# The first four rows of w1 as blocks, the sums of batch 1 on VectorE, and other costs in the planner's model

## The chip, the cores and the metric

The kernel runs on one core of a Trainium2 chip. The metric is the time of one execution on the device in microseconds (us). PE is the matrix engine (TensorE), DVE is VectorE, ACT is ScalarE, POOL is GpSimd, and SP issues all DMAs.

## The reference

Three blocks follow each other, on 4 batches of 448 tokens with 768 features:

```python
scores = cap * tanh(q @ k.T / 8 / cap)          # 12 heads of 64, per batch
attn = exp(scores - max); attn /= sum(attn) + 1e-9
x = attn @ v                                    # [4, 448, 768]

xn = (x - mean(x)) / sqrt(var(x) + 1e-6) * g_ln # the FFN
x = x + relu(xn @ w_ch1) @ w_ch2                # 768 -> 3072 -> 768

h = relu(x @ w_in); u, v = halves of h          # the gated block, 1024 = 2 * 512
v_s = w_spatial @ layernorm(v) + b_spatial
out = (u * v_s) @ w_out
```

Everything is in float32. The large weights come to the chip as 64-bit floats, in two 32-bit words each.

## The kernel before

**Stages.** The batches go in pairs. The attention of batches 0 and 1 leads the program: 24 heads, two to a step, so that the indices i are 0, 2, .. 22 (i = 12 is the first of batch 1). Then the FFN's first product runs for batches 0 and 1 (`h_units`, 24 rows of w1, of 128 hidden features each), with the attention of batches 2 and 3 and the conversion of w2 beside it. The second product follows in a form with seven products for eight (`y_seven`), then the gated block (`gmlp`), and then the same for batches 2 and 3.

**Precision.** A large product is made of three matmuls in fp32r: a value is split into a high and a low part (`cp` and `sub`), and hi*hi, hi*lo and lo*hi are summed in PSUM. Attention uses plain fp32 matmuls, of which the trace shows two records each.

**Attention that leads.** `lead_s` makes the scores of three chunks of 128 keys, in two pairs of PSUM banks (`twos`) and one more pair (`t3`), and takes tanh and exp on ScalarE into a tile E. The remaining 64 keys of two steps are made together in `lead_st` into a tile et. `lead_v` adds E's chunks on VectorE into s, multiplies by v, copies the result out as x, and sums s over the partitions with a matmul by ones, into a bank `pr`. Two steps share one such bank, except for the last two (i = 20, 22). A last matmul by `sel`, which has ones for one half of the partitions, adds the sums of et. For i in DIRECT (14, 18, 20, 22) E's third chunk isn't added on VectorE but summed by a matmul of its own. The sums go through DRAM to be inverted and spread over partitions (those of i = 22 are inverted in place), and `emit_n` multiplies x by them.

**Layer norm.** For batch 0 `x_done` adds the six x tiles into `acc` on VectorE; `feature_sum` splits acc and sums it over the partitions by two matmuls in fp32r. For batch 1 (MEANS) `direct_sum` sums the six x tiles by six fp32 matmuls. `ln_center` subtracts the mean, multiplies by g, splits each of the six tiles into xn, and adds up the squares; `ln_scale` makes the variance, whose root only scales x and comes in later.

**The first product.** `h_units` takes four rows of w1 first, then two at a time. For each batch and row `h_unit` sums 18 matmuls (six tiles k of three) in one bank. After the first such unit of batch 0 the mean and the centring of batch 1 are put in. The first four rows of w1 are converted and split ahead, during the attention (`make`), two of them into tiles of the pool rs: a Prelu on ScalarE rebases the upper word, VectorE shifts it and puts in the bits of the lower word.

**PSUM.** There are two pairs of banks (`twos`) and two single `banks`; two more single banks come when `t3` is given back after the last step's scores.

**The order.** No engine's order is written out by hand. Every call is recorded with a cost and a latency (`Recorder.record`), in the order of the program; `order` gives each operation a due time from the PE time before it, and `plan` simulates the five engines' queues and hands out, for each engine that is free, the ready operation that is due first, if its tiles fit into the pools. The result is issued in that order. `attend` gives the times, in matmuls of the first product, at which the stages of a head enter the program; `drive` mixes them with `h_units`. AFTER[2] is the part of that product over which the 24 heads of batches 2 and 3 are spread, and `total` is 24 rows by 36 matmuls.

The profile puts every operation on L568, the call in `record`; it is told apart by its tiles. The changed constants are at L37 to L58, `plan` is at L367, `record` at L539, `make` at L724, `value` at L736, `lead_v` at L878, `x_done` at L974, the layer norm at L1102 to L1160, `h_units` at L1795, `attend` at L1829.

Of the kernel before, what the change touches and what calls it, by code (L numbers as in the profile page):

```python
# [42 lines left out]
SECOND = 0  # L43
DIRECT = 14, 18, 20, 22
SQUARES = ()
MEANS = 1,
# [5 lines left out]
REST = 7, 9  # L52
# [4 lines left out]
SWITCH = 0.17  # L57
NEAR = 3.0  # L58
# [168 lines left out]
class Program:  # L227
# [139 lines left out]
    def plan(self, due):  # L367
# [85 lines left out]
        while True:  # L453
            for e in ready:
# [24 lines left out]
                for j, at in succ[i]:  # L479
                    heapq.heappush(events, (max(now, done - at), 1, seq, j))  # L480
                    seq += 1
# [47 lines left out]
class Recorder:  # L529
# [3 lines left out]
    def __getattr__(self, method):  # L533
# [5 lines left out]
        def record(*args, **kw):  # L539
# [24 lines left out]
            if self.name == "V":  # L564
                cost += 0.06 * sum(hasattr(kw.get(k), "tensor") for k in ("scalar", "scalar1", "scalar2"))

# [10 lines left out]
def attn_ffn_gmlp_kernel(  # L577
# [146 lines left out]
    def make(kind, j):  # L724

        with prog.early():

            made[kind, j] = weight(kind, j, [rs.get().rearrange("p a n -> p (a n)") for _ in range(2)]
# [7 lines left out]
    def value(kind, j, home=None, pool=wr):  # L736
# [8 lines left out]
        else:  # L745
# [5 lines left out]
            A.activation(out=t, in_=hi.bitcast(F32), func=ACTF.Prelu, scale=REBASE, alpha=-(2.0 ** 32))  # L751
            if home is None and kind in ("wv", "wu", "wo"):
# [3 lines left out]
            else:  # L756
                V.tensor_scalar(out=ti, in0=ti, scalar1=3, scalar2=None, op0=ALU.logical_shift_left)
                V.scalar_tensor_tensor(out=ti, in0=lo, scalar=29, in1=ti, op0=ALU.logical_shift_right,
# [119 lines left out]
    def lead_v(i):  # L878
# [5 lines left out]
        parts = [s]  # L884
        if i in DIRECT:
            parts.append(E[:, 2])
        else:
            add(s, s, E[:, 2])
        x = xts[b][h // 2]
        todo.append((i, parts, x, et))  # L890
# [15 lines left out]
        if now:  # L906
            with prog.group():
                most = max(len(a) for _, a, _, _ in now)
                for m in range(most + 1):
                    for n, (j, a, _, e) in enumerate(now):  # L910
                        if m < most and m >= len(a):
                            continue
                        for half in range(2):
                            q = (2 * n + half) * width
                            T.matmul(out=pr[q:q + width], lhsT=sel[:, j // 2 % 2, 0:width] if m == most else ones128[:, 0:width],
                                     rhs=(e if m == most else a[m])[:, half], start=m == 0, stop=m == most)
# [57 lines left out]
    def x_done(b, h, x):  # L974
        k = h // 2
        if b in MEANS:
            return
# [133 lines left out]
    def direct_sum(ps, xs):  # L1111

        for k, x in enumerate(xs):
            with prog.group():
                T.matmul(out=ps, lhsT=ones128, rhs=x, start=k == 0, stop=k == KD - 1)

    means = {}

    def ln_mean(b):
        ps = banks.get()[:, 0:S]  # L1120
        if b in MEANS:
# [673 lines left out]
    def h_units(bs):  # L1795

        j0 = 0
        for m in (4, *[2] * (NF // 2 - 2)):
            w = [weight("w1", row(j0 + j)) for j in range(m)]
            mine = {}  # L1800
            for b in bs:
                for j in range(m):
# [4 lines left out]
                    if b in ln and j == 0:  # L1807
                        ln_scale(b)
# [142 lines left out]
```

## Time and profile before

| | |
|---|---|
| median of 3 runs | 1025.92 us (1025.5 to 1026.25) |
| the profiled execution | 1024.53 us |
| its span, first to last instruction | 1022.4 us |
| PE busy | 1006.7 us, 5130 matmuls |
| VectorE busy | 840.0 us, 1447 instructions |
| ScalarE busy | 554.0 us, 850 instructions |
| DMA | 248.71 MB, 70.9% of 16 engines' span |

Times in the trace are counted from the first instruction. A matmul's duration holds its way through the array, so that a stream of them starts at shorter distances than each one takes; "PE busy" is the union of them. Where one row of the timeline is followed by the next row of the same engine, the distance of the two starts is what the first one took of the engine's time.

### The profile page before, as it was taken

To read this page: it belongs to the slowest core of one execution; us is meant where nothing else is said; L and a number is where in the kernel's file an instruction comes from. 1 tells how busy PE (TensorE), PEld (TensorE's weight loads), DVE (VectorE), ACT (ScalarE), POOL (GpSimd) and SP (SyncE) were. 2 spreads that over 40 slices of the span, in tenths; PEclk is the share of its full clock that TensorE was granted. 3 is DMA by queue.
4 is the path that set the end of the run, shared out by engine and by line. 5 is a ranking of instruction groups with operands and counts; after the bars stand their busy time and mean duration, and the time that the engine had idled before them with its cause. 6 is when DMAs were issued, how large, how long until landed. Compare 5 with 4: busy or idle time off the path is not lost.

```text
span 1022.4 us, 15003 instructions
## 1 busy us (share of the span) xinstructions
PE 1006.7 (98%) x5130; PEld 830.9 (81%) x5130; DVE 840.0 (82%) x1447; ACT 554.0 (54%) x850; POOL 17.8 (2%) x21
## 2 busy tenths in 40 slices
PE   7999999999999999999999999999999999999998
PEld 2334687788778889999989899999989999998887
DVE  3869889878868879988889999888788777778996
ACT  7996866776576444455555345444554322214553
POOL 0000000000000000000001110000000000000000
PEclk9999999999999999999999999999999999999999
DMA  6646689999999999989774233566799987602402
GB/s 209 207 142 178 206 283 342 362 353 380 337 346 346 361 346 400 409 321 359 260 249 158 50 132 116 162 202 200 251 332 375 323 261 236 189 23 69 132 16 108
DMA packets 131759, 248.71 MB, mean 243 GB/s; under 512 B 21682, under 2 KB 93540, under 8 KB 131684
## 3 DMA queue, kind: packets, MB, share of 16 engines
q1 hardware_dynamic: 131684, 247.76, 70.9%
q8 instruction: 40, 0.66, 0.2%
q14 instruction: 35, 0.29, 0.1%
HBM read 167.70 MB, written 80.01 MB: 242 GB/s over the span
## 4 chain that ended last, share of the span: by engine, by line
PE 78%; DMA 11%; DVE 4%; ACT 3%; SPq 1%; issue 1%; DVEq 0%; ACTq 0%
PE bank L568 51%; PE two L568 26%; DMA kept_w<-wr 2%; ACT e L568 2%; DMA w<-in_w_dram 2%; SPq L568 1%; DMA hs<-inv 1%; DMA kept_w<-wc 1%; DMA qk<-in_qk_dram 1%; DVE small L568 1%; DMA x<-hs 1%; DMA h<-hx 1%; DVE rs L568 1%; ACT es L568 1%; PE t L568 1%
## 5 line engine op out<-in xcount | busy, mean ns | idle before, releaser
L568 PE MATMUL bank<-rs,wh 128*128 128x448 f32 x1704 | 356.9, 363 | 1.3 <-ACT hs L568 1.3
L568 PEld LDWEIGHTS bank<-rs,wh 128*128 128x128 f32 x1704 | 318.3, 187 | 28.5 <-ACT hs L568 3.7
L568 DVE TENSOR_TENSOR rs<-hs,rs 128x448 fp32r<-128x448 f32 x159 | 94.6, 620 | 3.8 <-ACT rs L568 3.7
L568 PE MATMUL two<-rs,wh 128*128 128x448 f32 x414 | 92.7, 362 | 0.0
L568 ACT ACTIVATE rs<-hs 128x448 fp32r<-128x448 f32 x126 | 68.1, 569 | 31.4 <-DMA hs<-h 25.7
L568 PEld LDWEIGHTS two<-rs,wh 128*128 128x128 f32 x414 | 77.6, 188 | 5.2
L568 DVE TENSOR_TENSOR wh<-wr,wh 128x768 fp32r<-128x768 f32 (+2 forms) x72 | 62.4, 866 | 4.6 <-ACT wh L568 4.2
L568 ACT ACTIVATE wh<-wr 128x768 fp32r<-128x768 f32 (+2 forms) x53 | 40.8, 770 | 30.5 <-DVE wr L568 14.2
L568 ACT ACTIVATE hs<-bank 128x448 f32<-128x448 f32 x56 | 30.1, 540 | 33.0 <-PE bank L568 29.1
L568 ACT ACTIVATE wc<-w 128x512 f32<-128x512 f32 x36 | 24.1, 673 | 38.4 <-DMA kept_w<-wc 20.4
L568 ACT ACTIVATE es<-es,capt 128x896 f32<-128x896 f32 x42 | 42.3, 1048 | 0.0
L568 PE MATMUL two<-qk 64*128 64x448 f32 (+1 forms) x168 | 36.0, 593 | 4.1 <-DMA qk<-in_qk_dram 4.1
L568 ACT ACTIVATE rs<-x 128x448 fp32r<-128x448 f32 x34 | 19.1, 575 | 32.3 <-DVE x L568 31.0
L568 PE MATMUL bank<-es,vt 128*64 128x448 f32 (+1 forms) x192 | 35.6, 551 | 0.3 <-ACT es L568 0.3
L568 PE MATMUL two<-wh,rs 128*128 128x512 f32 x144 | 35.6, 395 | 0.0
L568 ACT ACTIVATE wh<-wqm 128x768 fp32r<-128x768 f32 x19 | 16.1, 846 | 32.7 <-PE bank L568 20.8
L568 ACT ACTIVATE es<-two,qsc 128x896 f32<-128x896 f32 x32 | 31.9, 1011 | 3.4 <-PE two L568 3.4
L568 PE MATMUL bank<-rx,whb 128*128 128x448 f32 x144 | 32.7, 362 | 0.0
L568 PE MATMUL two<-rx,whb 128*128 128x448 f32 x144 | 32.7, 362 | 0.0
L568 PEld LDWEIGHTS two<-qk 64*128 64x128 f32 (+1 forms) x168 | 12.4, 180 | 24.8 <-issue 8.7
L568 PEld LDWEIGHTS two<-wh,rs 128*128 128x128 f32 x144 | 26.9, 187 | 6.7 <-DVE rs L568 0.2
L568 PE MATMUL bank<-e,vt 128*64 128x448 f32 x144 | 29.9, 548 | 1.9 <-ACT e L568 1.7
(247 smaller groups left out, 1953.5 us busy)
## 6 DMA issues: line engine op xcount, KB each, us to landing
hs<-h SPq DMA_DIRECT2D x168, 224.0 KB, 5.5
h<-hx SPq DMA_DIRECT2D x84, 224.0 KB, 6.0
w<-in_w_dram SPq DMA_DIRECT2D x24, 768.0 KB, 5.5
w<-in_w_dram SPq DMA_DIRECT2D x36, 512.0 KB, 6.1
wqm<-kept_w SPq DMA_DIRECT2D x30, 384.0 KB, 6.1
qk<-in_qk_dram SPq DMA_DIRECT2D x24, 448.0 KB, 5.1
h<-hs SPq DMA_DIRECT2D x48, 224.0 KB, 3.7
kept_w<-wr SPq DMA_DIRECT2D x24, 384.0 KB, 7.4
```

Of the source, the lines that this page charges most:

```text
L568: fn(*(put(a) for a in args), **{k: put(a) for k, a in kw.items()})
```

## The change

The constants change, with a cost PIPE that `record` takes off the cost of VectorE's and ScalarE's instructions and adds to their latency; in `plan` a PE operation that follows another one of PE is released when that one's cost is over. In `lead_v` all three chunks are added on VectorE, the tails of heads under TAILS too, and the matmul by `sel` stays for the others. In `value` the four rows that are made ahead are rebased by VectorE. Batch 1's mean goes the way of batch 0's (the code of DIRECT, MEANS and of the empty SQUARES goes). `h_units` makes the first four rows in one block per batch, over the tiles k, in two single banks and one pair; the mean and the centring of batch 1 come after tile k = 1 of batch 0. The attention of batches 2 and 3, but for its first scores, is put START matmuls later and spread over what is left. The pools es and hx, of REST tiles, change from 7 and 9 to 6 and 11. LOW names all six rows of each of its kinds.

```diff
@@ -40,21 +40,23 @@
 LEAD_ST = 0.12
 MAKE = 3.1
 LN_AT = 3.2
-SECOND = 0
-DIRECT = 14, 18, 20, 22
-SQUARES = ()
-MEANS = 1,
+SECOND = 1
+START = 76
+TAILS = 12
+HOME = 1
+LOW = {"wv": range(6), "wu": range(6), "wo": range(6)}
 
 FAST = 22,
 
 COUNTS = 16, 10, 3, 2, 3, 1
 FIRST = 2, 2, 2, 2
-REST = 7, 9
+REST = 6, 11
 LEAD = 2, 6
 
 
 AHEAD = 28
 SWITCH = 0.17
+PIPE = 0.07
 NEAR = 3.0
 SLACK = 0.35
 BIAS = 0.1
@@ -477,7 +479,8 @@
                 heapq.heappush(events, (now + cost, 0, seq, e))
                 done = now + cost + latency + self.DELAY
                 for j, at in succ[i]:
-                    heapq.heappush(events, (max(now, done - at), 1, seq, j))
+                    same = e == "PE" and self.ops[j][0][0][0] == "PE"
+                    heapq.heappush(events, (now + cost if same else max(now, done - at), 1, seq, j))
                     seq += 1
                 heapq.heappush(events, (done, 2, seq, i))
                 seq += 1
@@ -563,6 +566,9 @@
                 cost = 0.14 + n / 960
             if self.name == "V":
                 cost += 0.06 * sum(hasattr(kw.get(k), "tensor") for k in ("scalar", "scalar1", "scalar2"))
+
+            if self.name in "VA":
+                cost, latency = cost - PIPE, PIPE
 
             def call():
                 fn(*(put(a) for a in args), **{k: put(a) for k, a in kw.items()})
@@ -725,7 +731,7 @@
 
         with prog.early():
 
-            made[kind, j] = weight(kind, j, [rs.get().rearrange("p a n -> p (a n)") for _ in range(2)]
+            made[kind, j] = weight(kind, j, [rs.get().rearrange("p a n -> p (a n)")[:, 48:] for _ in range(2)]
                                    if j < 2 else [t[:, i] for t in (wh.get(),) for i in range(2)])
 
     def ahead(kind, j):
@@ -748,13 +754,19 @@
             t = pool.get()[:, 0:n]
             ti = t.bitcast(I32)
             hi, lo = raw[:, :, 1], raw[:, :, 0]
-            A.activation(out=t, in_=hi.bitcast(F32), func=ACTF.Prelu, scale=REBASE, alpha=-(2.0 ** 32))
-            if home is None and kind in ("wv", "wu", "wo"):
+            if home is None or not HOME:
+                A.activation(out=t, in_=hi.bitcast(F32), func=ACTF.Prelu, scale=REBASE, alpha=-(2.0 ** 32))
+            else:
+                V.tensor_scalar(out=t, in0=hi.bitcast(F32), scalar1=REBASE, scalar2=None, op0=ALU.mult)
+            if home is None and kind in LOW and j % 6 in LOW[kind]:
                 A.activation(out=lo, in_=lo.bitcast(U32), func=ACTF.Copy, scale=TOP, bias=FLOOR)
                 V.scalar_tensor_tensor(out=ti, in0=ti, scalar=3, in1=lo, op0=ALU.logical_shift_left,
                                        op1=ALU.bitwise_or)
             else:
                 V.tensor_scalar(out=ti, in0=ti, scalar1=3, scalar2=None, op0=ALU.logical_shift_left)
+                if home is not None and HOME:
+                    V.scalar_tensor_tensor(out=ti, in0=hi, scalar=-(1 << 31), in1=ti, op0=ALU.bitwise_and,
+                                           op1=ALU.bitwise_or)
                 V.scalar_tensor_tensor(out=ti, in0=lo, scalar=29, in1=ti, op0=ALU.logical_shift_right,
                                        op1=ALU.bitwise_or)
             if kind == "w2":
@@ -881,13 +893,12 @@
         u, E, et = raws["v", i], st.pop(i), st.pop(("t", i))
         s = es0.get()
         add(s, E[:, 0], E[:, 1])
-        parts = [s]
-        if i in DIRECT:
-            parts.append(E[:, 2])
-        else:
-            add(s, s, E[:, 2])
+        add(s, s, E[:, 2])
+        p = place(i)
+        if i < TAILS:
+            add(s[p], s[p], et[p])
         x = xts[b][h // 2]
-        todo.append((i, parts, x, et))
+        todo.append((i, s, x, et))
         now = todo[:] if i // 2 % 2 or alone(i) else []
         ps = tails[i] if i in tails else banks.get()[:, 0:S]
         for ns in [range(3)] if i else [[n] for n in range(3)]:
@@ -905,15 +916,12 @@
         width = 64 if len(now) == 1 else 32
         if now:
             with prog.group():
-                most = max(len(a) for _, a, _, _ in now)
-                for m in range(most + 1):
+                for last in range(1 if i < TAILS else 2):
                     for n, (j, a, _, e) in enumerate(now):
-                        if m < most and m >= len(a):
-                            continue
                         for half in range(2):
                             q = (2 * n + half) * width
-                            T.matmul(out=pr[q:q + width], lhsT=sel[:, j // 2 % 2, 0:width] if m == most else ones128[:, 0:width],
-                                     rhs=(e if m == most else a[m])[:, half], start=m == 0, stop=m == most)
+                            T.matmul(out=pr[q:q + width], lhsT=sel[:, j // 2 % 2, 0:width] if last else ones128[:, 0:width],
+                                     rhs=(e if last else a)[:, half], start=not last, stop=bool(last) or i < TAILS)
         if not now:
             return
         todo.clear()
@@ -973,8 +981,6 @@
 
     def x_done(b, h, x):
         k = h // 2
-        if b in MEANS:
-            return
         if k == 0:
             accof[b] = accs[b % 2].get()
         acc = accof[b]
@@ -1108,20 +1114,11 @@
             for j in range(2):
                 T.matmul(out=ps, lhsT=onesr, rhs=t[:, j], start=(j == 0), stop=(j == 1))
 
...
     means = {}
 
     def ln_mean(b):
-        ps = banks.get()[:, 0:S]
-        if b in MEANS:
-            direct_sum(ps, xts[b])
-        else:
-            feature_sum(ps, accof[b], rs if b >= 2 else wh)
+        ps = twos.get()[:, 0, 0:S] if b == 1 else banks.get()[:, 0:S]
+        feature_sum(ps, accof[b], rs if b >= 2 else wh)
         means[b] = rst[b % 2] if b >= 2 else hs.get()
         A.activation(out=means[b], in_=ps, func=ACTF.Copy, scale=1.0 / DM)
 
...
@@ -1794,18 +1781,35 @@
 
     def h_units(bs):
 
-        j0 = 0
-        for m in (4, *[2] * (NF // 2 - 2)):
+        w = [weight("w1", row(j)) for j in range(EARLY)]
+        mine = {}
+        for b in bs:
+            two = twos.get()
+            pss = [banks.get()[:, 0:S] for _ in w[2:]] + [two[:, j, 0:S] for j in range(2)]
+            for k, x in enumerate(xn[b]):
+                with prog.group():
+                    for (hi, lo), ps in zip(w, pss):
+                        for m, (l, r) in enumerate(((hi, x[:, 0]), (hi, x[:, 1]), (lo, x[:, 0]))):
+                            T.matmul(out=ps, lhsT=l[:, k], rhs=r, start=k == 0 and m == 0,
+                                     stop=k == KD - 1 and m == 2)
+                if b == bs[0] and k == SECOND:
+                    ln_mean(1)
+                    ln_center(1)
+            for j, ps in enumerate(pss):
+                mine[b, j] = hx.get()
+                relu(mine[b, j], ps)
+            ln_scale(b)
+            yield 3 * KD * EARLY
+        for j in range(0, EARLY, 2):
+            h = [mine[e, i] for i in (j, j + 1) for e in bs]
+            mixed_h(j // 2, *h, *(hx.get() for _ in range(3)))
+        j0 = EARLY
+        for m in [2] * (NF // 2 - 2):
             w = [weight("w1", row(j0 + j)) for j in range(m)]
             mine = {}
             for b in bs:
                 for j in range(m):
                     mine[b, j] = h_unit(b, w[j])
-                    if j0 == 0 and (b, j) == (0, SECOND):
-                        ln_mean(1)
-                        ln_center(1)
-                    if b in ln and j == 0:
-                        ln_scale(b)
                     if b % 2 and j % 2:
                         h = [mine[e, i] for i in (j - 1, j) for e in bs]
                         mixed_h((j0 + j) // 2, *h, *(hx.get() for _ in range(3)))
@@ -1826,11 +1830,11 @@
         for _, fn, args in todo:
             fn(*args)
 
-    def attend(first, n, per):
+    def attend(first, n, per, start=0.0):
         todo = []
         for j in range(0, n, 2):
             i = first + j
-            t = per * j
+            t = per * j + start
 
             stages = [(S_AT[0] if i >= 2 * SPLIT else 0.0, emit_s, i, (0, 1)),
                       (S_AT[1] if i >= 2 * SPLIT else 0.1, emit_s, i, (2,)), (LOAD_QK, emit_load, i + 4),
@@ -1845,7 +1849,7 @@
                 stages += [(4.2, emit_n, i)]
             elif i // 2 % 2:
                 stages += [(4.2, emit_n, i - 2), (4.2, emit_n, i)]
-            todo += [(t + x * per, fn, a) for x, fn, *a in stages]
+            todo += [(t + x * per - (start if j == 0 and x < 0.2 else 0.0), fn, a) for x, fn, *a in stages]
         return todo
 
     def main():
@@ -1879,7 +1883,7 @@
             later = [("wv", k) for k in range(KD)] + [("wu", i) for i in range(KH)] + [("wo", k) for k in range(KD)]
             todo = [(total * (AFTER[0] + (AFTER[1] - AFTER[0]) * j / len(rows)), ahead, x) for j, x in enumerate(rows)]
             n = 2 * H
-            drive(h_units(bs), todo + attend(n, n, AFTER[2] * total / n))
+            drive(h_units(bs), todo + attend(n, n, (AFTER[2] * total - START) / n, START))
             raw6[:] = w6m, wcm, w6m
             y_seven(wqm, later)
             gmlp(bs, [2 * p + 2, 2 * p + 3])
```

## Rows read from the trace of the kernel before

**Rows 1.** The page: busy us of the engines, their share, instructions.
```profile
PE 1006.7 (98%) x5130; PEld 830.9 (81%) x5130; DVE 840.0 (82%) x1447; ACT 554.0 (54%) x850; POOL 17.8 (2%) x21
```
**Rows 2.** The chain that ended last, merged: start, us, engine and tile, instructions.
```profile
418.61 22.80 PE bank L568 x114
```
**Rows 3.** PE's waits: us in total, times, longest.
```profile
PE bank L568 <- ACT e L568: 1.7, 2, 1.4
...
PE two L568 <- ACT whm L568: 1.6, 1, 1.6
```
**Rows 4.** Busy time by engine, the sum over four stretches from 24.34 to 79.65.
```profile
sum 55.31, PE 54.86 PEld 19.00 DVE 41.08 ACT 53.37 POOL 0.00; mean PE 13.71 PEld 4.75 DVE 10.27 ACT 13.34 POOL 0.00
```
**Rows 5.** VectorE's groups up to 100 us: count, busy us, mean ns, idle before, releasers.
```profile
L568 DVE TENSOR_TENSOR es<-e 128x896 f32<-128x896 f32 x12 | 13.1, 1089 | 14.9 <-ACT e L568 14.8
...
L568 DVE SCALAR_TENSOR_TENSOR wr<-w,wr 128x768 int32<-128x768 int32 x4 | 3.8, 962 | 0.1
...
L568 DVE TENSOR_SCALAR wr<-wr 128x768 int32<-128x768 int32 x4 | 2.2, 557 | 1.3 <-ACT wr L568 1.3
...
L568 DVE CAST wh<-acc 128x448 fp32r<-128x448 f32 x1 | 0.4, 394 | 0.0
```
**Rows 6.** Busy time by engine from 85 to 125 us, with clock and DMA.
```profile
85.00:125.00 40.00, 40.00 (x196) 22.44 (x193) 33.13 (x60) 27.76 (x43) 1.02 (x1) 1.00 0.59 189
```
**Rows 7.** PE's timeline, 50 to 67 us: start, us, operation, count.
```profile
52.77 0.94 PE L568 MATMUL bank<-es,sel 128*32 128x448 f32 x8
53.63 1.77 PE L568 MATMUL two<-qk 64*128 64x448 f32 x8
...
65.06 0.55 PE L568 MATMUL bank<-e,onesr 128*32 128x448 f32 x2
...
66.66 0.61 PE L568 MATMUL two<-qk 64*64 64x448 f32 x4
```
**Rows 8.** PE's timeline, 79 to 130 us.
```profile
87.55 0.92 PE L568 MATMUL bank<-e,onesr 128*64 128x448 f32 x4
88.31 0.92 PE L568 MATMUL bank<-es,sel 128*64 128x448 f32 x4
...
98.58 1.02 PE L568 MATMUL bank<-x,onesr 128*128 128x448 f32 x2
...
99.84 0.91 PE L568 MATMUL bank<-x,onesr 128*128 128x448 f32 x2
100.69 1.77 PE L568 MATMUL two<-qk 64*128 64x448 f32 x8
...
110.51 1.02 PE L568 MATMUL bank<-x,onesr 128*128 128x448 f32 x2
111.02 4.15 PE L568 MATMUL bank<-rs,rs 128*128 128x448 f32 x18
...
124.68 3.98 PE L568 MATMUL bank<-rs,rs 128*128 128x448 f32 x18
128.49 0.57 PE L568 MATMUL bank<-wh,onesr 128*128 128x448 f32 x2
128.90 1.36 PE L568 MATMUL bank<-rs,wh 128*128 128x448 f32 x6
```
**Rows 9.** ScalarE's groups up to 100 us, the Prelu of the early rows.
```profile
L568 ACT ACTIVATE wr<-w 128x768 f32<-128x768 f32 x4 | 3.8, 944 | 0.0
```
**Rows 10.** ScalarE's timeline, 12 to 26 us.
```profile
14.02 0.92 ACT L568 ACTIVATE wr<-w 128x768 f32<-128x768 f32 x1
```
**Rows 11.** VectorE's timeline, 84 to 130 us.
```profile
103.90 1.16 DVE L568 TENSOR_TENSOR x<-x,hs 128x448 f32<-128x448 f32 x2 [2.21 <-DMA hs<-inv]
```
**Rows 12.** PE's timeline at the border to the second product, 365 to 382 us.
```profile
373.71 0.68 PE L568 MATMUL two<-rs,whm 128*128 128x448 f32 x2 [1.61 <-ACT whm L568]
375.16 3.85 PE L568 MATMUL two<-rs,whm 128*128 128x448 f32 x10 [0.77 <-DVE whm L568]
```
**Rows 13.** Busy time by engine there, with PE's granted clock behind POOL.
```profile
375.20:378.60 3.40, 3.40 (x9) 3.05 (x10) 3.10 (x5) 2.51 (x3) 0.00 (x0) 0.50 1.01 346
```

More of the change, by code (lines that the diff above doesn't have):

```diff
@@ L1109, in feature_sum @@
                 T.matmul(out=ps, lhsT=onesr, rhs=t[:, j], start=(j == 0), stop=(j == 1))
[L1111 to L1115, printed above, removed]
     means = {}
     def ln_mean(b):
-        ps = banks.get()[:, 0:S]
-        if b in MEANS:
-            direct_sum(ps, xts[b])
-        else:
-            feature_sum(ps, accof[b], rs if b >= 2 else wh)
+        ps = twos.get()[:, 0, 0:S] if b == 1 else banks.get()[:, 0:S]
+        feature_sum(ps, accof[b], rs if b >= 2 else wh)
         means[b] = rst[b % 2] if b >= 2 else hs.get()
@@ L1128, in ln_center @@
     def ln_center(b):
-        mean, sq = means.pop(b), None if b in SQUARES else hs.get()
+        mean, sq = means.pop(b), hs.get()
         xn[b] = []
@@ L1142, in ln_center @@
             xn[b].append(t)
-            if b in SQUARES:
-                A.activation(out=u, in_=u, func=ACTF.Square)
-                squares.setdefault(b, []).append(u)
-                continue
             A.activation(out=u if k else sq, in_=u, func=ACTF.Square)
@@ L1150, in ln_center @@
         ln[b] = sq
-    squares = {}
     def ln_scale(b):
-        ps = banks.get()[:, 0:S]
-        if b in SQUARES:
-            ln.pop(b)
-            direct_sum(ps, squares.pop(b))
-        else:
-            feature_sum(ps, ln.pop(b))
+        ps = twos.get()[:, 0, 0:S]
+        feature_sum(ps, ln.pop(b))
         row = hs.get()[0:1]
```

## The prediction, made before the changed kernel ran

> **What bounds the kernel now.** I read the page first, then PE's chain and waits, the busy time by stage, PE's own timeline, and last the groups of VectorE and ScalarE in the attention that leads the program. PE is busy 1006.7 us, 98% of the span [rows 1]. A busy PE may still be slow, so I looked at its pace: a stretch of 114 matmuls takes 22.80 us, 0.20 each [rows 2], and such stretches make up the chain that ends last. Of its waits, after the first load, only two come to more than a microsecond at a time: 1.4 us once for ScalarE's exponentials and 1.6 us once for a split weight [rows 3]. So the time is the length of PE's own work plus few stalls, and work taken off PE shortens the program as far as the others keep up.
>
> In the first 85 us they hardly do. From the sums of heads 0 and 2 to those of heads 16 and 18 are 55.31 us, four pairs of heads; in them PE is busy 54.86, ScalarE 53.37 and VectorE 41.08 [rows 4]. ScalarE, at 96%, is a second bound. VectorE has 14 us left; 14.9 us it waits for ScalarE before the first adds of the sums [rows 5]. From 85 to 125 PE has no gap, VectorE is busy 33.13 and ScalarE 27.76 of 40 [rows 6].
>
> **What the change takes off PE.** For heads under 12 the tail's sums go to VectorE, and the step with sel goes. The step that starts at 52.77 is followed at 53.63 [rows 7]: 0.86; the two others are like it (0.87 and 0.97), together 2.70 us. For heads 14, 18, 20 and 22 the products of E's third chunk with the ones go. The pair with such products runs from 65.06 to 66.66 [rows 7], 1.60 where 0.86 would be left, so 0.75; there are two such pairs, and heads 20 and 22 pay as much each (87.55 to 88.31 [rows 8]): 3.0 us. The mean of batch 1 was six fp32 products: three take 0.85 to 0.95 (99.84 to 100.69) and three 0.51 (110.51 to 111.02), 4.17 in all; two products like those from 128.49 to 128.90, 0.41, replace them [rows 8]: 3.76 us. The sum is 9.46 us. 3.45 of it lies in the four pairs (three sel steps and head 14's 0.75), 6.0 behind them.
>
> **What the others lose and gain.** ScalarE loses four passes over 768, 944 ns each [rows 9]. Two are in the four pairs: 53.37 becomes 51.5. Of the two ahead, the one at 14.02 [rows 10] stands in the exponentials for which PE waits the 1.4 us; I take 1.0 us back there, between nothing and the 1.7 us of both waits [rows 3].
> VectorE gains six tail adds, on 64 partitions by 896, put at the 1.09 of the 128x896 adds; four adds of the third chunk, 1.09 each; in four rows of w1 a scaling and a bit operation; for batch 1 a copy and five adds into acc, and the split of the sum by a cast (0.39) and a subtraction (0.62, as other operations over 448 [rows 5, 11]). The bit operation is like the one at 0.962. The scaling isn't in the trace: nearest is the shift over the same 768 with one input, 0.557; the upper end is the 0.962 of an operation that reads the same strided half. I take 0.56, the row of the same kind of instruction. 6.5 + 4.4 + 6.1 + 4.5 = 21.5 us, at most 23.1. The Trainium skill ("VectorE: DVE Perf Modes", Mode 2×_2P) has fp32 operations with one source run two elements a cycle where source and destination lie in SBUF and the outermost dimension is even, which a strided source doesn't spoil; by it the sum is 21.5, without it 23.1. The trace agrees for the contiguous case (0.557 against 0.962); no run here shows the strided one.
>
> In the four pairs VectorE's part is four tail adds (4.4), head 14's add (1.1), three rows of w1 (4.6) and two steps of acc (1.0): 11.1. Two operations of 0.62 in a row take 1.16 [rows 11], so each of some 13 hides 0.08: 41.08 + 11.1 − 1.1 is 51. PE has 55.31 − 3.45 = 51.9, ScalarE 51.5: three engines level. Until now ScalarE filled 96.5%; at that, 52 us take 53.9, a gain of 1.4. Ends: 3.45 if PE's loss comes through whole, and −1.2 if three level engines fill only 92% (56.5). The change adds a wait here: a pair's sums stand behind the exponential of its tails, which sel took later; behind that add on VectorE are queued the copy of x and the next sums, and PE's product with the ones waits for it.
>
> Behind the four pairs VectorE, at 33.13 of 40, gets 2.2 for heads 20 and 22, 2.5 of acc and 1.0 of the split, and is rid of what batch 2's attention asked of it there, which now comes 76 products later. PE has batch 0's four rows to fill in, 72 products or 14.4 us, as before. I take the 6.0 as whole, with 3 as the low end.
>
> **The blocks** are the same 144 products in another order, at 0.20 each either way: nothing. What hides the making of batch 1's mean is batch 0's block; a block also starts with the first centred tile, where a unit wanted all six within 3.6 us. Without that cover it costs what the last rival says. The moved offset in rs touches two of the four rows: their 18 products take 3.81 (124.68 to 128.49 [rows 8]) against 18 times 0.20, so four units could give 0.8 at most; I count nothing. One es buffer fewer, two hx more, the denser later attention and the planner's new costs reorder everything behind 125 us and add or remove no work there: nothing, ±3, as the pauses there could go or grow by about that.
>
> **Sum.** 6.0 + 1.4 + 1.0 = 8.4 us. The profiled execution took 1024.53, 2.1 outside its span; less 8.4 it is 1016.1. The median of the runs, 1025.92, is 1.4 above that execution: 1025.92 − 8.4 = **1017.5**. Own range 1015 to 1021.
>
> **Rivals.** *All of it, and the pause at the stage border too.* PE gives 9.5. Before 373.71 it waits 1.61 us for a split weight and before 375.16 another 0.77, and the ten products from there take 3.85 us instead of 2.0 [rows 12], at a granted clock of 0.50 [rows 13], the lower of its two levels, 1.2 GHz: 2.4 of pause and 1.9 of slow clock. The later attention ends some 7 products earlier by its placing. Against it: the pause ended with a split behind its load, and those loads stay. 1025.92 − 9.5 − 4.3 is 1012.
> *VectorE becomes the lead's bound.* Its adds wait for ScalarE already, and now more stands behind each. If the four pairs fill only 90%, they take 57.8, 2.5 more than before; if 3 us of the 6.0 are lost the same way and the 1.0 at the start comes, the gain is 1.5: 1024.5. For it: 51 of 52 us. Against it: ScalarE lost work, and copies out of PSUM may go to it.
> *Slower: PE runs dry while batch 1's mean is made.* From the end of head 22's sums (98.58) to batch 1's first product (124.68) are 26.1 us [rows 8], filled with three units of batch 0, the fp32 mean and attention of batch 2. A block holds two banks and half a pair of them, the fp32 mean is gone, and attention beyond its first scores (4.4) is put off; 14.4 + 4.4 + 0.4 = 19.2 us are left. If the chain keeps its length PE idles 6.9, acc, cast and split add 1.6, a slow clock as in [rows 13] 1.9: 10.4 lost against 8.4 won, 1028. It decides from some 8 us of idle on. Against it: the last inputs of the mean were there at 105 (x times 1/sum from 103.90 [rows 11]) and its last product came at 110.51 only because PE was busy; the chain by itself wants some 12 us. The Trainium skill ("TensorE: Matmul & The Clock Gate", Why this matters for your kernels) warns that idle stretches between bursts cost clock; the trace agrees at the 0.50 above.
> *The change doesn't do what it says*: the new costs order the later stages worse by what the lead gains, near 1025.9.
>
> **Chances.** Forecast 0.5; all and more 0.2; VectorE the bound 0.11 (half of it within 0.2% of before); nothing gained 0.05; slower 0.11; 0.03 for more still. Range 1011 to 1026: all but the slower case and the far end. A measurement of this kernel can't tell less than 0.2% (2.05 us) from no change: faster by over that 0.79, within it 0.10, slower 0.11.
>
> **What would show it.** The x,onesr and e,onesr groups leave PE and half of es,sel; VectorE's instructions before 125 us rise by some 20 and it is over 90% busy there; PE's waits before 85 us stay under 3 us; the four pairs end 2 to 3 us earlier and batch 1's first product comes by 117. Wrong would be PE's waits of several us for VectorE's es or acc before 125, an unchanged length of the four pairs, or a longer stretch from 125 us to the stage border.

## The result: slower by 0.8%

The changed kernel takes 1034.07 us (median of 6 runs, 1030.2 to 1037.87) against 1025.77 for the kernel before beside it: a ratio of 1.0081, 95% interval 1.0061 to 1.0101. I had forecast 1017.5 and a range that ended at 1026. The profiled execution took 1032.76 us, its span 1031.0.

PE's line of the page (columns as in [rows 1]):

```profile
PE 1004.1 (97%) x5080; PEld 830.9 (81%) x5080; DVE 870.0 (84%) x1505; ACT 534.7 (52%) x817; POOL 11.4 (1%) x18
```

The work left PE as forecast: 50 matmul records fewer. Busy time hides how much that is, since a matmul at the slow clock is busy for longer. So I count each matmul of the trace at the distance of two starts in an undisturbed stretch (0.200 us for 448 columns in fp32r, 0.233 for 512, 0.094 to 0.375 for the plain fp32 shapes) and call the sum PE's own work: 972.2 us before, 963.5 after, 8.7 less. What the span holds beyond it is lost: 50.2 us before, 67.5 after. The change won 8.7 us and lost 17.3 more. PE's waits (us in total, times, longest), which answer to [rows 3]:

```profile
PE two L574 <- DMA qk<-in_qk_dram: 5.5, 3, 3.9
PE two L574 <- ACT hs L574: 3.7, 2, 2.7
PE bank L574 <- ACT hs L574: 3.1, 1, 3.1
PE two L574 <- ACT es L574: 2.6, 1, 2.6
PE bank L574 <- DVE x L574: 2.1, 3, 1.3
```

Before, the first load's wait was 4.1 us, and no other was longer than 1.6. Busy time by stage (stretch; length, PE, PEld, VectorE, ScalarE, POOL; PE's granted clock, DMA share, GB/s):

```profile
24.76:80.05 55.29, 51.55 (x292) 17.40 (x291) 46.15 (x65) 50.42 (x46) 0.00 (x0) 1.00 0.52 159
...
85.00:125.00 40.00, 34.48 (x153) 21.69 (x150) 35.18 (x66) 25.58 (x41) 0.00 (x0) 0.87 0.49 155
```

The first is the four pairs: 55.29 us, where [rows 4] had 55.31; PE, VectorE and ScalarE all have slack. The second answers to [rows 6]: PE loses 5.5 us to waits and is slow besides. PE's timeline there, against [rows 8]:

```profile
107.36 0.47 PE L574 MATMUL two<-wh,onesr 128*128 128x448 f32 x1 [0.72 <-ACT wh L574]
108.02 0.47 PE L574 MATMUL two<-wh,onesr 128*128 128x448 f32 x1 [0.19 <-DVE wh L574]
...
111.36 0.45 PE L574 MATMUL two<-wh,onesr 128*128 128x448 f32 x1 [0.47 <-DVE wh L574]
112.34 0.47 PE L574 MATMUL two<-wh,onesr 128*128 128x448 f32 x1 [0.53 <-DVE wh L574]
113.83 2.57 PE L574 MATMUL two<-qk 64*128 64x448 f32 x8 [1.02 <-ACT hx L574]
119.00 1.87 PE L574 MATMUL two<-qk 64*128 64x448 f32 x4 [2.60 <-ACT es L574]
120.80 1.49 PE L574 MATMUL bank<-rs,rs 128*128 128x448 f32 x3
```

Batch 1's first product starts at 120.80 (before 124.68, forecast by 117), but before it PE stands, and three products take 1.49 us, not 0.76. After the five waits of 0.2 to 1.0 us from 107 on, the granted clock from 114.5 to 124.7 us is the lower level, 1.2 GHz, as in [rows 13]; it is so again from 169 us, in another wait:

```profile
114.50:124.70 10.20, 7.60 (x21) 4.34 (x20) 8.71 (x17) 8.46 (x14) 0.00 (x0) 0.51 0.14 47
169.00:176.00 7.00, 5.64 (x22) 2.99 (x23) 5.57 (x10) 6.41 (x10) 0.22 (x1) 0.52 0.96 333
```

What PE waits for stands in ScalarE's queue behind something else. ScalarE's timeline (in brackets its idle time and what ended it):

```profile
109.43 0.89 ACT L574 ACTIVATE wr<-w 128x768 f32<-128x768 f32 x1 [2.13 <-DMA w<-in_w_dram]
110.22 0.54 ACT L574 ACTIVATE hs<-two 128x448 f32<-128x448 f32 x1
...
116.37 0.66 ACT L574 ACTIVATE wc<-w 128x512 f32<-128x512 f32 x1 [1.60 <-DMA w<-in_w_dram]
116.94 0.65 ACT L574 ACTIVATE rs<-hs,g_t 128x448 fp32r<-128x448 f32 x1
117.49 0.56 ACT L574 ACTIVATE hs<-hs 128x448 f32<-128x448 f32 x1
117.96 1.89 ACT L574 ACTIVATE es<-two,qsc 128x896 f32<-128x896 f32 x2
...
168.97 0.91 ACT L574 ACTIVATE wr<-w 128x768 f32<-128x768 f32 x1 [5.10 <-DMA w<-in_w_dram]
169.77 0.54 ACT L574 ACTIVATE hs<-bank 128x448 f32<-128x448 f32 x1
...
957.74 0.63 ACT L574 ACTIVATE rbc<-vtc 128x512 fp32r<-128x512 f32 x1 [2.94 <-DVE vtc L574]
958.78 1.22 ACT L574 ACTIVATE rbc<-vtc 128x512 fp32r<-128x512 f32 x2 [0.42 <-DVE vtc L574]
959.91 0.52 ACT L574 ACTIVATE hs<-two 128x448 f32<-128x448 f32 x1
```

hs<-two at 110.22 is batch 1's mean, es<-two at 117.96 frees the bank for which PE waits 2.60, hs<-bank at 169.77 frees the one for which it waits 3.07, hs<-two at 959.91 the one of 2.67. Each time ScalarE had been idle for 1.6 to 5.1 us with a weight's conversion or a late cast at its head, and PE's bank behind it. Two loads of 512 KB for wc are long on the way, by the chain of waits (start, us, what):

```profile
99.49 5.48 DMA w<-in_w_dram
...
109.26 7.03 DMA w<-in_w_dram
```

### The profile page after: what moved, and what is told of

Its sections match the earlier page's. It is cut to its first block, busy times and chain, and to the rows that moved or that the text cites. A ratio compares the mean times of both kernels' runs of the same rounds, so it can differ in the third digit from the quotient of the medians.

```text
span 1031.0 us, 14905 instructions
## 1 busy us (share of the span) xinstructions
PE 1004.1 (97%) x5080; PEld 830.9 (81%) x5080; DVE 870.0 (84%) x1505; ACT 534.7 (52%) x817; POOL 11.4 (1%) x18
## 4 chain that ended last, share of the span: by engine, by line
PE 79%; DMA 8%; DVE 6%; ACT 3%; issue 1%; SPq 1%; POOL 0%; ACTq 0%; DVEq 0%; POOLq 0%
PE bank L574 54%; PE two L574 25%; DMA w<-in_w_dram 3%; ACT e L574 1%; DVE x L574 1%; DVE small L574 1%; SPq L574 1%; DMA var_t<-var 1%; DVE es L574 1%; DMA qk<-in_qk_dram 1%; DMA rc<-sum 1%; DMA wr<-kept_wo 1%; DMA x<-x 1%; DMA inv<-rc 1%; ACT es L574 1%
## 5 line engine op out<-in xcount | busy, mean ns | idle before, releaser
L574 PE MATMUL bank<-rs,wh 128*128 128x448 f32 x1668 | 352.7, 364 | 0.3 <-DVE rs L574 0.3
L574 PEld LDWEIGHTS bank<-rs,wh 128*128 128x128 f32 x1668 | 312.5, 188 | 28.2 <-issue 3.3
L574 PE MATMUL two<-rs,wh 128*128 128x448 f32 x450 | 103.5, 366 | 3.7 <-ACT hs L574 3.7
L574 PEld LDWEIGHTS two<-rs,wh 128*128 128x128 f32 x450 | 85.4, 190 | 10.2 <-ACT hs L574 4.4
L574 ACT ACTIVATE rs<-hs 128x448 fp32r<-128x448 f32 x108 | 59.1, 569 | 30.9 <-DMA hs<-h 20.2
L574 ACT ACTIVATE wh<-wr 128x768 fp32r<-128x768 f32 (+2 forms) x46 | 35.3, 767 | 16.1 <-PE bank L574 6.2
L574 ACT ACTIVATE wh<-wqm 128x768 fp32r<-128x768 f32 x19 | 16.1, 846 | 43.1 <-PE bank L574 26.3
L574 DVE TENSOR_TENSOR es<-es,es 128x896 f32<-128x896 f32 (+1 forms) x30 | 32.7, 1088 | 4.4 <-ACT es L574 3.9
L574 PEld LDWEIGHTS two<-qk 64*128 64x128 f32 (+1 forms) x168 | 12.9, 185 | 28.6 <-issue 10.7
L574 ACT ACTIVATE whb<-wrb 128x768 fp32r<-128x768 f32 x24 | 20.3, 846 | 23.7 <-PE two L574 20.2
```

Of the source, the lines that this page charges most:

```text
L574: fn(*(put(a) for a in args), **{k: put(a) for k, a in kw.items()})
```

## The experiments

Theory A: the blocks, with the attention of batch 2 put off, leave PE without work at 106 to 121 us. B: VectorE is too full in the lead. C: the planner's costs put instructions into in-order queues ahead of their data, and what PE needs stands behind. D: the border to the second product waits for w2's bytes. E, formed later: whatever the costs, an order that is drawn anew loses some 45 us or more somewhere. Each group of runs had the kernel before beside it (medians 1025.67 to 1026.58 us). The table gives the ratio to the kernel before (3 rounds, 5 from e14 on), PE's own work and what is lost up to the first product of the second stage and after it, the last three from the profiled execution.

| | median us | ratio (95%) | own | lost to border | lost after |
|---|---|---|---|---|---|
| before | 1025.8 | | 972.2 | 35.4 | 14.9 |
| changed | 1034.07 | 1.0081 (1.0061-1.0101) | 963.5 | 50.4 | 17.1 |
| e1 no blocks | 1033.5 | 1.0074 (1.0048-1.0099) | 963.5 | 48.6 | 22.2 |
| e2 no sums | 1043.04 | 1.0188 (1.0155-1.0221) | 972.2 | 45.3 | 19.5 |
| e3 old costs | 1027.62 | 1.0020 (1.0001-1.0040) | 963.5 | 47.2 | 16.4 |
| e4 START 0 | 1030.82 | 1.0052 (1.0036-1.0068) | 963.5 | 44.2 | 20.1 |
| e5 sums only | 1026.91 | 1.0003 (0.9980-1.0025) | 963.5 | 45.3 | 16.1 |
| e6 + half w2 | 1032.16 | 1.0058 (1.0038-1.0078) | 963.5 | 51.5 | 16.7 |
| e7 costs only | 1031.42 | 1.0053 (1.0025-1.0081) | 972.2 | 37.5 | 22.6 |
| e8 PIPE only | 1032.0 | 1.0065 (1.0040-1.0091) | 972.2 | 38.9 | 18.6 |
| e9 bn_stats | 1027.57 | 1.0021 (0.9998-1.0043) | 963.5 | 50.7 | 11.6 |
| e10 landing | 1026.15 | 1.0003 (0.9984-1.0022) | 963.5 | 43.8 | 19.2 |
| e11 old costs, early end | 1028.59 | 1.0029 (1.0007-1.0051) | 963.5 | 48.6 | 14.3 |
| e12 sums, early end | 1025.22 | 0.9987 (0.9964-1.0010) | 963.5 | 45.6 | 12.5 |
| e13 w2 once | 1033.83 | 1.0064 (1.0040-1.0088) | 963.5 | 46.3 | 18.8 |
| e14 both costs | 1021.8 | 0.9972 (0.9955-0.9989) | 963.5 | 43.4 | 11.8 |
| e15 sums, end, bn_stats | 1027.01 | 1.0003 (0.9989-1.0018) | 963.5 | 44.9 | 16.7 |
| e16 before, bn_stats | 1029.08 | 1.0027 (1.0010-1.0044) | 972.2 | 39.2 | 20.0 |
| e17 before, both costs | 1036.98 | 1.0101 (1.0086-1.0116) | 972.2 | 46.0 | 16.4 |
| e18 sums, both costs | 1032.09 | 1.0049 (1.0036-1.0062) | 963.5 | 51.1 | 16.6 |

**The parts, one taken out of the changed kernel at a time.** e1 has `h_units` as before and REST 7, 9, SECOND 0, START 0, and it takes the sums of batch 1's mean and of the variances in a single bank again (the change takes them in a pair of `twos`; its diff shows that for the mean alone); e2 has DIRECT, MEANS and the Prelu back; e3 has PIPE 0 and the old release in `plan`; e4:

```diff
-START = 76
+START = 0
```

> The changed kernel with its first four rows as single units again (mean of batch 1 after the first unit, the attention of batches 2 and 3 not put off, es and hx at 7 and 9); the sums on VectorE and the planner's new costs stay. Theory A (the blocks and the late attention leave PE without work from 106 to 121 us): this wait goes, some 9 to 10 us with its slow clock, and the time is 1022 to 1026, with no wait of PE over 2 us between 95 and 130. Theory B (VectorE has too much in the lead): 1030 to 1034, the waits at 55 and 62 us stay and the mean of batch 1 still comes late. Theory C (the new costs order worse): 1030 to 1036, the waits at 167 and 957 us stay.

> The changed kernel with the tails, the third chunks, the mean of batch 1 and the Prelu of the early rows back on PE and ScalarE; blocks, late attention and new costs stay. Theory A: the wait from 106 us stays, shorter by the 3.8 us for which PE makes the fp32 mean, and PE has 9.5 us more work: 1034 to 1040. Theory B: the lead's waits go and the mean is early: 1024 to 1028. Theory C: 1034 to 1042.

> The changed kernel with PIPE at 0 and every PE operation released with its latency, as before; blocks, late attention and the sums on VectorE stay. Theory A: 1030 to 1037, the wait from 106 us is there, the ones at 167 and 957 us may move. Theory B: 1030 to 1037. Theory C: 1020 to 1026, since with the old costs nothing is put ahead of its data.

> The changed kernel with START at 0: the attention of batches 2 and 3 enters as early as before; blocks and all else stay. Theory A, if the missing filler is the attention: the wait from 106 us falls by 4 us or more, 1026 to 1030. If it is the block itself, which holds two banks and a pair and so keeps the scores of batch 2 out: the wait stays within 2 us, 1031 to 1036. Theories B and C: no change, 1030 to 1037.

Without blocks the loss between 100 and 125 us falls from 11.4 to 1.5 us, although batch 1's first product starts at 119.27, hardly earlier than 120.80: the mean comes almost as late, and PE has other work meanwhile. So A and the place were right; but the time stays (A had 1022 to 1026), since PE now waits elsewhere (e1's PE at batch 1's first product and at the border, the latter against [rows 12], where 1.61 stood):

```profile
119.27 3.88 PE L578 MATMUL bank<-rs,rs 128*128 128x448 f32 x18
...
378.31 5.32 PE L578 MATMUL two<-rs,whm 128*128 128x448 f32 x12 [5.70 <-ACT whm L578]
```

e4, with the later attention in its old place, loses 6.7 us at 100 to 125 and 6.5 at the border instead. Without the sums the kernel is 9.0 us slower than changed, 1 us above the highest range: PE's own work is back at 972.2, and B, which had 1024 to 1028, falls (VectorE 46.15 of 55.29 in the four pairs). With the old costs it is 6.5 us faster, 1.6 us short of C's range: the waits behind 950 us and at 573 are gone, as C has it, but one of 5.6 us comes at the border.

**One part alone, put into the kernel before.** e5 is the kernel before with the sums on VectorE, e7 with the new costs, e8 with PIPE alone. e6 is e5 in which the odd rows of w2 are made from the raw words of the even row before (their loads left out):

```diff
+            if kind == "w2" and j % 2:
+                raw = half["w2"]
```

> The kernel before with only the sums moved to VectorE (tails, third chunks, batch 1's mean, the rebasing of the early rows); first rows as units, old costs. PE loses 9.5 us of work. Theory D (the border to the second product opens when the DMA queues are through with w2 and the attention's loads, at 368 to 374 us in every run so far, whatever PE does before): PE comes there at 362 to 364 and waits 8 to 11 us, then runs some microseconds at the slow clock, and the time is 1022 to 1027. Without D: no longer wait there than the 2.4 us of before, and 1016 to 1019.

> As the run with the sums only, but every odd row of w2 is converted from the raw words of the row before it, so that 18 loads of 512 KB are left out (9.4 MB; the odd rows' values are thus wrong). Theory D: the border opens some 8 to 25 us earlier, PE finds its weights there, the wait and its slow clock are gone: 1013 to 1018. Without D: within 2 us of the run with the sums only.

> The kernel before with only the planner's new costs (PIPE 0.07 and PE's operations released at the end of the one before). PE's work is that of before. Theory C (the new costs put instructions into ScalarE's queue ahead of their data, and what PE waits for stands behind them): the waits at 573 and 957 us come back, 1.5 and 2.8 us with 1.5 of slow clock, and 1.2 near 1009, 5 to 6 us in all: 1030 to 1034, more if the stage before the border is hit too. If the costs only do harm together with the sums or the blocks: 1025 to 1028.

> The kernel before with PIPE 0.07 alone, PE's operations released as before. If it is the lower cost of VectorE and ScalarE that puts instructions ahead of their data: 1030 to 1034 with the wait of 2.8 us near 957. If it is the earlier release on PE: 1025 to 1027 and no such wait.

e5 has 8.7 us less to do and gains nothing: 9.9 us more are lost before the border, above all 4.9 at 25 to 85 us, 3.7 at 100 to 125 without any block (5.9 against 2.2) and 3.4 at 125 to 150. Its time lies in D's range, but PE's wait at the border is 1.84 us, not 8 to 11. e6 reaches the border at 381.2, later than e5 (375.1), and is slower than both its ranges, so D falls. e7 and e8 are slow with no work added: PIPE is the cost that matters. In e8, PE behind 950 us:

```profile
958.89 2.67 PE L578 MATMUL two<-rs,wh 128*128 128x448 f32 x9 [2.67 <-ACT hs L578]
```

ScalarE's queue there is that of the changed kernel, 1.6 us earlier: rbc<-vtc at 956.14 after 2.94 us of idle time, hs<-two at 958.31. The casts rbc<-vtc wait for VectorE, whose bn_stats take longer than the planner has them. Its cost goes by the output, 6 elements: 0.14 + 6/960 = 0.146 us, less PIPE 0.076; in the changed kernel (group, count, busy us, mean ns; the 0.62 us in the expectation of e9 is too low):

```profile
L574 DVE BATCH_NORM_STATS2 small<-vtc 128x6 f32<-128x512 f32 x7 | 4.6, 679 | 0.0
```

**The costs corrected.** e9 and e10 are the changed kernel with one cost mended; e11 (from e3) and e12 (from e5) end the later attention sooner instead:

```diff
-            n = out.free_size()
+            n = kw["in_"].free_size() if method == "bn_stats" else out.free_size()    # e9
-                    latency = moved + 0.77 - now - cost
+                    latency = moved + 2.5 - now - cost                                # e10
-AFTER = 0.05, 0.9, 0.93
+AFTER = 0.05, 0.9, 0.87                                                               # e11, e12
```

> The changed kernel with one more cost put right in the model: bn_stats is charged for the 512 elements it reads, not the 6 it writes (0.62 us each in the traces against 0.15). Theory C (the model's too early ends put ScalarE's casts of the normalised rows ahead of the copy that PE waits for): the waits at 573 and 957 us go back to the 0.8 of before, with their slow clock, 4 to 6 us in all, and the waits before 380 us stay as they are: 1027 to 1031. If those waits have another cause: 1031 to 1037, and the 2.8 us stay.

> The changed kernel with every DMA's landing in the model 1.73 us later (0.77 to 2.5). If the waits at 106 to 121 and at 167 us come from conversions that the model puts into ScalarE's and VectorE's queues before their loads of w1 and w2 have landed (5.5 to 7 us in the traces), they shrink by half or more and PE's loss from 100 to 175 us falls from 19 us to 10: 1023 to 1028. If they come from the blocks' lack of other work for PE alone, the 100 to 125 us stay as they are and only 167 goes: 1029 to 1032.

> The changed kernel with the old costs, and the attention of batches 2 and 3 spread over 0.87 instead of 0.93 of the first product. If the wait at the border (5.8 us and 3 us of slow clock with the old costs) is for the inversion of the last heads' sums, ahead of which no weight of the second product is loaded, it goes, since the sums come 9 us earlier: 1018 to 1022. If the border is held by the DMA queues as a whole, the wait stays over 4 us: 1025 to 1030.

> The kernel before with only the sums on VectorE and the attention of batches 2 and 3 spread over 0.87. By the same reason the border's wait of 2 us and its slow clock go, but the waits of 100 to 150 us stay: 1022 to 1026. If the denser attention costs more than the border gives: 1027 to 1031.

e9 wins 6.5 us back. ScalarE's queue there has the copy first, and PE has no gap:

```profile
955.46 0.55 ACT L578 ACTIVATE hs<-two 128x448 f32<-128x448 f32 x1 [1.25 <-PE two L578]
957.17 0.63 ACT L578 ACTIVATE rbc<-vtc 128x512 fp32r<-128x512 f32 x1 [1.17 <-DVE vtc L578]
```

That is C shown at one place. e10 wins 7.9 us, but not as C had it: the wait at 170 goes, and the gap at 106 to 121 only changes its name (5.7 us for wh at 111.87, 11.2 lost), which was the sign named for the blocks; the loss shrinks elsewhere. e11 has 2.3 us left of the border's 5.6 and is over 6 us above the range for that; in e12 the border's wait is gone, and it gains nothing that can be told from none: an earlier end draws another order too.

**The gap at 106 to 121 us, and all of it together.** e13 is the changed kernel with rows 1 to 11 of w2 made from row 0's raw words; e14 has both corrections; e15 is e12 with bn_stats corrected, e16 the kernel before with that alone:

```diff
+            if kind == "w2" and 0 < j < 12:
+                raw = once["w2"]
```

> The changed kernel, in which rows 1 to 11 of w2 are made from row 0's raw words, so that 11 loads of 512 KB between 90 and 150 us are left out (the output is not the reference's). Theory C (ScalarE's queue stands behind loads that land late): with these loads gone the w1 rows land sooner and nothing waits for w2, so batch 1's first product comes by 117.5 us (changed kernel 120.80), PE loses less than 6 us between 100 and 125 (11.4 there), and the time is 1025 to 1030. Theory A (the blocks leave PE without work, whatever the loads do): first product at 119.5 or later, 9 us or more lost, 1031 to 1036.

> The changed kernel with both corrections of the order's costs, bn_stats by what it reads and a load's landing 1.7 us later. Theory C (the stalls come of costs that are too small): the corrections add, the waits behind 950 us and at 167 us both stay away, 1017 to 1024. Theory E (each change of a cost draws another order, and an order drawn anew loses some 45 us somewhere whatever the costs): one group of waits goes and another comes, 1024 to 1031.

> The kernel before with the sums on VectorE, the later attention ending at 0.87 of the stage and bn_stats charged by what it reads; no blocks, none of the change's costs. Theory C: nothing is lost against the same without the bn_stats charge (1025.22) and the gap behind 569 us shrinks, 1020 to 1024. Theory E: 1021 to 1030, with waits of 2 us or more at places where neither kernel had them.

> The kernel before with bn_stats charged by what it reads and nothing else. Theory C: its own order already has the copies ahead of the casts behind 950 us, so there is little to win: 1023 to 1026.5. Theory E: 1022 to 1031, PE's waits moved to other places, its own work unchanged at 972.

e13, PE and ScalarE in that stretch:

```profile
111.36 1.77 PE L578 MATMUL two<-qk 64*128 64x448 f32 x8 [1.02 <-ACT hx L578]
114.84 1.02 PE L578 MATMUL two<-qk 64*128 64x448 f32 x4 [1.70 <-ACT es L578]
115.79 0.87 PE L578 MATMUL bank<-rs,rs 128*128 128x448 f32 x3
```

```profile
112.18 0.68 ACT L578 ACTIVATE wc<-w 128x512 f32<-128x512 f32 x1
```

The blocks are all there, ScalarE no longer waits for a load at 112, batch 1's first product starts at 115.79, inside C's forecast, and 4.6 us are lost instead of 11.4. So the gap has two conditions: loads that land late ahead of ready work make the mean take 5 us longer, and the blocks leave PE without work meanwhile (e1). Its 11.4 us can't be shared out between them: without the sums 3.5 us are lost there, without the blocks 1.5, with START at 0 6.7, with the old costs 6.0, and these gains and e13's are three times what there is. Two of PE's waits there (1.02 and 2.60) end when a pair of `twos` is given back; whether the sums that the change takes in such a pair add to the gap is untested. The time of e13 was not C's 1025 to 1030 but inside A's 1031 to 1036: the wait of 3.07 us at 170 comes back as one of 3.3 at 196, and the ones behind 950 stay.

e14 is the first version below the kernel before: 1021.8, ratio 0.9972 (0.9955 to 0.9989). PE's line of its page, and then its longest waits:

```profile
PE 997.2 (98%) x5080; PEld 826.8 (81%) x5080; DVE 864.1 (85%) x1493; ACT 540.0 (53%) x829; POOL 11.7 (1%) x18
```

```profile
PE two L578 <- DVE wh L578: 6.4, 2, 5.7
PE two L578 <- DMA qk<-in_qk_dram: 4.0, 1, 4.0
PE bank L578 <- ACT e L578: 3.0, 3, 1.6
```

The corrections nearly add (6.5 and 7.9, together 12.3), and the waits at 170 and 957 stay away; the gap at 106 us does not. e15 and e16 are in E's ranges and above C's: the charge for bn_stats that won 6.5 us in the changed kernel won nothing against e12 and lost 2.7 against the kernel before.

**Whose gain it is.** The same corrections without the change, and with the sums alone:

> The kernel before with both corrections of the order's costs (bn_stats by what it reads, a load's landing 1.7 us later) and no part of the change. If the 4.6 us that the changed kernel with both has on the kernel before come of the change's work off PE, this one stays at 1024 to 1030, 2 us or more behind it; if they come of the corrected costs alone, it is at 1018 to 1023. PE's own work stays 972 us.

> The kernel before with the sums on VectorE and both corrections of the order's costs; no blocks, none of the change's own costs. If the blocks and the change's costs carry nothing of the gain, this one is within 3 us of the changed kernel with both (1021.8): 1019 to 1025. If they carry it, 1025 to 1030, near the sums alone (1026.9). Theory E (an order drawn anew loses as it happens) puts it anywhere from 1019 to 1030, with PE's own work at 963.5 and 55 to 66 us lost.

The kernel before gets 10.4 us worse by them, above both ranges, so the corrections alone don't give e14's gain. e17 at the border, PE's timeline:

```profile
368.49 3.48 PE L578 MATMUL bank<-rs,wh 128*128 128x448 f32 x16 [0.32 <-DVE wh L578]
384.30 5.07 PE L578 MATMUL two<-rs,whm 128*128 128x448 f32 x12 [12.33 <-DMA wqm<-kept_w]
```

and SP's queue, where those loads stand behind the copies hs<-h:

```profile
372.24 3.00 SPq L578 DMA_DIRECT2D hs<-h  x6
...
378.52 7.55 SPq L578 DMA_DIRECT2D wqm<-kept_w  x10
```

So a truer cost isn't a better order by itself, as E has it. Under the same corrected costs the kernel with the sums is 4.9 us faster than without (1036.98 to 1032.09, above all its ranges), and the rest of the change takes off 10.3 more (to 1021.8; by the ratios 5.3 and 7.9); under the old costs the sums gained nothing (e5). What stays open is whether e14 is C's gain or a good draw: the waits at 170 and 957 are gone from it, but one kernel can't tell the two apart, and no order other than the planner's was tried.

## Why the prediction was wrong

**PE's work, 9.46 us: right.** 8.7 counted in the trace; e2, which puts the work back, has all of it again.

**VectorE's terms: right or high.** The scaling that no trace had shown takes 557 ns (4 of them 2.2 us) from a source of every second word, as the contiguous shift does: the value I took, 0.56. The Trainium skill ("VectorE: DVE Perf Modes", Mode 2×_2P) asks for one source, SBUF and an even outermost dimension, not for a contiguous source; the trace agrees. In the four pairs VectorE rose by 5.1, not 10, to 46.15: one of the four scalings falls into that stretch, where I had three rows of w1. Up to 125 us it is busy 81% of the time, not over 90%.

**The four pairs, 1.4: wrong, 0.** I asked whether the engines are full; none is (51.55, 46.15 and 50.42 of 55.29). PE lost 10.5 us there, before 6.4, and 3.7 of them in waits, before none: it waited for two things that no busy share shows, loads of qk (the longest 1.34 at 56.89) and VectorE's x (1.27 at 64.00), and VectorE had been held by the inverted sums:

```profile
58.42 0.62 DVE L574 TENSOR_TENSOR x<-x,hs 128x448 f32<-128x448 f32 x1 [1.39 <-DMA hs<-inv]
...
62.24 0.24 DVE L574 RECIPROCAL rc<-rc 128x14 f32<-128x14 f32 x1 [1.09 <-DMA rc<-sum]
62.40 1.03 DVE L574 TENSOR_TENSOR es<-e 128x896 f32<-128x896 f32 x1
```

Work that waits for a DMA stands ahead of a sum that is ready. The 1.0 at the start came: PE's product behind that wait starts at 20.49, before at 21.93, and up to the first sums 9.7 us are lost, before 10.7. The wait itself is as long as it was (1.38 us, before 1.40), as PE gets there earlier too; how much of the 1.0 is the Prelu's no run tells.

**"I take the 6.0 as whole": the first step that failed.** The cover that I named for batch 1's mean, batch 0's block, ran out; my slower rival had the place, and idle time plus slow clock near its 10.4 (11.4 us lost between 100 and 125, before 2.2). What I set against that rival failed: I put the chain of the mean by itself at some 12 us from the end of head 22's sums, by its own operations' lengths, and forgot the loads of w1 and w2 in the same queues. It took 25.2 us (95.64 to 120.80), 12.5 of them two such loads by the chain of waits, and without eleven loads of w2 PE lost 4.6 us instead of 11.4 (e13). A block also takes two single banks and a whole pair, not half of one. At 0.11 the rival had too little, with a price that nearly fits.

**"Everything behind 125 us: nothing, ±3": the second.** From 125 us to the border 3.0 us more than before are lost (6.4 more at 150 to 175, less elsewhere), and 2.2 behind it; the other 12 lie before 125. The new costs alone cost 5.5 to 6.1 us against the kernel before beside them (e7, e8). My rival *The change doesn't do what it says* had that too, at 0.05 and as if it stood alone. What came, by the count, was both rivals less the gain: 1025.8 − 8.7 + 17.3 = 1034.4. Two of the signs of being wrong were there: the four pairs' unchanged length, and 255.1 us from 125 us to the border, before 248.7. Of the first rival only the border came true: PE's product at 380.09 starts without a wait and at the full clock, where 2.4 us of pause and 1.9 of slow clock were before.

**What stays open.** Why the sums alone gain nothing: e5, with neither blocks nor new costs, loses 11.1 us more than the kernel before, and the two longest waits between its lead and the border (2.46 us for a load of qk at 122.40, 1.62 for ScalarE's hs at 131.68) are less than half of that. Taking away one cause at a time (e1, e4, e13) didn't bring the time back, as the new order lost elsewhere what the old one had lost here.

## What to carry to other kernels

Where a planner writes the order of in-order queues, a change of its costs or of any operation's length is a new order: price it at what the planner's orders differ by (here 55 to 71 us lost among eighteen near relatives, 50 in the kernel before, and medians from 1021.8 to 1043), not only at the sum of the moved work. Read a queue's head, not its busy share: an idle engine with a load's consumer at its head is a full engine to all that stands behind. And before a new cost model is trusted, lay its costs beside the trace's durations operation by operation (0.076 against 0.679 us for bn_stats), but measure the order that comes of it: the kernel before got 10.4 us slower with truer costs (e17).

## What the runs showed of the hardware

Two loads of 512 KB landed 5.5 and 7.0 us after their issue (99.49 and 109.26 us); the DMA engines were 0.86 and 0.83 busy meanwhile, at 260 and 254 GB/s. ScalarE stood idle for 1.6, 2.1 and 5.1 us with the conversion of such a load, or of one of 768 KB, at the head of its queue. The Trainium skill ("DMA: Bandwidth & Descriptors", Rules for kernel authors) says to issue a transfer early and wait for it late; here the wait itself came early, in a queue. PE's clock fell to 0.51 after five waits of 0.2 to 1.0 us, stayed there through one of 2.60 and came back 10.2 us after it fell. Of the 11.4 us lost between 100 and 125 us only 5.5 are waits; of the rest some 3.8 are the clock (an estimate: half of the 7.60 us for which PE was busy at the lower level).
